# Output projection of a fused fp32 kernel: seven block products over all three input quads, and ten clamps moved to GpSimd

## The chip, the cores and the metric

The kernel runs on one core of a Trainium2 chip. The metric is the device time of one execution in microseconds (us). A core has a matrix engine (TensorE, PE in the rows, with its weight loads as PEld), a vector engine (VectorE, DVE), an activation engine (ScalarE, ACT), a general engine (GpSimd, POOL) and SyncE (SP), whose queue starts the transfers from and to memory. Each engine works through its own instructions in order; semaphores make one engine wait for another.

## The reference

```
attn_out = attention(q_pool, k, v)            # 2 x 8 heads, pooled queries
x = attn_out laid out as (1152 tokens, 512)
h = x @ w_in;  g = elu(h);  x = g @ w_out     # 512 -> 2048 -> 512
xn = x / sqrt(mean(x*x) + 1e-6) * rms_g
g = xn @ w_gate;  val = xn @ w_val            # 512 -> 1536
out = (silu(g) * val) @ w_out                 # 1536 -> 512, the output projection
```

Everything is float32 to full precision. The change concerns the last line, whose left factor is called u below.

## The kernel before

**One product in three.** TensorE multiplies in a reduced format, so each operand is held as a high part and a low part (the rest), and each 128x128 weight block times 128x384 activations takes three matmuls: high·high, low activations·high weights, high activations·low weights (L236 to L238). The activations are kept with the token on the free axis, in three chunks of 384 tokens.

**The output projection.** The 512 output rows are four row blocks m of 128. The inner axis of 1536 is three *quads* of 512, and a quad is four blocks of 128. So the plain product has 4 row blocks x 3 chunks x 3 quads = 36 products of a weight piece (row block, quad) with a quad of u, each 4 x 3 = 12 matmuls. For chunks 0 and 1 and quads 0 and 1 the kernel uses a scheme with seven block products in the place of eight, once for each pair of row blocks, which takes two products off: 34 products, 408 matmuls. The seven need four sums s1 to s4 of weight pieces (`combine_own`, L169) and four differences t1 to t4 of quads of u (`sum_t`, L1159, DVE, 128x1536 each). Every activation that enters TensorE is split: ScalarE casts the high part, DVE (or GpSimd, `lo_pool`) subtracts to get the low part (`split_x`, `split_t`, L1115 to L1125). The buffers xh/xl and th/tl (`tsh`/`tsl` in rows) are used again and again for these parts.

**The weight stream.** `Stream.work` (L101) decodes 68 pieces; the last twelve, W0 to W11 here, belong to the output projection. A piece arrives as 128x512 pairs of 32-bit words, 512 KB, in one of two buffers `wr`. ScalarE turns the low words into a count `we` (L121) and takes the absolute value of the high words into `wm`, a tile in PSUM (L123). DVE clamps `wm` (L132), ors the count in (L134) and sets the sign (L137), which frees the `wr` buffer for the next load. ScalarE casts the high part `wh` (L198), and GpSimd subtracts to get `wl` (L64). `ws.step(i, k)` at a place of the program puts the next k steps of this decode there; `ws.get` puts all that is left until the piece is ready. So the order of all engines' queues is the order of the program's text.

**Sums of pieces.** For earlier weights GpSimd makes the four sums of a pair of pieces (`combine`, L155, four operations on 128x256), ScalarE casts them and GpSimd makes their low part (128x1024). The pairs W8/W9 and W10/W11 before go through `combine_own`: four DVE operations on 128x512 each (L174), which `round_s` splits later (`sumh`/`suml` in rows).

**The order at the end.** First the products that need only W0 to W3, then those with W4 to W7 as they come, then `ws.step(wi + 8, 40)`, which places the rest of the decode, then the plain products with W8 to W11 for chunk 2, and at last the rounds with sums: `sums[1]`, `sums[2]`, `sums[3]`, the pieces W9 and W11 themselves, and `sums[4]`. An evicted product goes to `o` (ScalarE or DVE, L1149) and from there to memory.

Of the kernel before, what the change touches and what calls it, by code (L numbers as in the profile page):

```python
# [22 lines left out]
CH = 384  # L23
# [16 lines left out]
def tile_kernel(ctx: ExitStack, tc: tile.TileContext, qd, kd, vd, w1d, w2d, wgd, wvd, wod, rgd, outd):  # L40
# [33 lines left out]
    class Stream:  # L74
# [26 lines left out]
        def work(self):  # L101
            tail = None
            for i in range(len(self.srcs)):
# [7 lines left out]
                if wide:  # L111
# [8 lines left out]
                    t = self.bank.tile([128, 512], U32, tag="wm", name="wm", bufs=1) if self.bank else w  # L120
                    T.activation(out=e, in_=lo, func=AF.Copy, scale=0.93625 * 2.0 ** -29)  # L121
# [23 lines left out]
                if i in self.keep:  # L145
                    T.copy(self.keep[i], w)
                    yield
# [5 lines left out]
            yield from tail  # L153

# [14 lines left out]
        def combine_own(self, i, a21, a22):  # L169

            s1, s2, s3, s4 = own[i]
            for o, a, b, op in ((s3, s3, a21, ALU.subtract), (s1, a21, a22, ALU.add),
                                (s2, a22, s3, ALU.subtract), (s4, s4, s2, ALU.subtract)):
                V.tensor_tensor(out=o, in0=a, in1=b, op=op)  # L174
                if o is s4:
                    self.own[i] = own[i]
# [14 lines left out]
        def split(self, i, w):  # L191
# [7 lines left out]
            yield  # L199
            lo_pool(l2, w, h2)  # L200
# [73 lines left out]
    last_pieces = [(0, 0), (1, 0), (0, 1), (1, 1), (0, 2), (1, 2), (2, 2), (3, 2), (2, 0), (2, 1), (3, 0), (3, 1)]  # L274
# [257 lines left out]
    def pair_of(i):  # L532
# [8 lines left out]
    ws.place = lambda n: sums_at[n % 2 if n < 8 else 1 if n == 8 else (n - 6) % 3]  # L541
# [434 lines left out]

    class Gate(Branch):
# [9 lines left out]
        def out(self, k, c, p, add=None, into=None):  # L987
            d = u[c][:, self.i + k]
# [22 lines left out]
    def swiglu(i, c, pg, pv, k=4):  # L1011
        s = u[c][:, i]
# [98 lines left out]
    c0, c1 = [at_t(6), at_t(10), at_t(2)], [None, at_x(1), at_x(2)]  # L1111
    c2 = [at_x(0), at_t(6), at_t(10)]
    t1, t2, t3, t4 = at_t(10), at_t(2), at_x(2), at_x(0)

    def split_x(l, w):  # L1115
        h, r = (t[:, 0:4, cs(l)] for t in (xh, xl))
        T.copy(h, w)
        lo_dve(r, w, h)

    def split_t(a, w):  # L1120
        for k in (0,) if a < 9 else (0, 2):
            n = 4 if a < 9 else 2
            h, r = (t[:, (a + k) % 12:(a + k) % 12 + n] for t in (th, tl))
            T.copy(h, w[:, k:k + n])
            lo_dve(r, w[:, k:k + n], h)  # L1125

    quad = lambda c, q: u[c][:, 4 * q:4 * q + 4]
# [182 lines left out]
```

## Time and profile before

| | us |
|---|---|
| median of three executions | 653.56 (655.15, 653.05, 653.56) |
| profiled execution, own time | 653.19 |
| its span | 651.4 |
| PE busy in the span | 643.7 (99%) |
| DVE busy | 542.3 (83%) |
| ACT busy | 468.0 (72%) |
| POOL busy | 443.4 (68%) |
| TensorE's granted clock, mean over the span | 1.00 |

The span is the time between the first and the last recorded instruction; the execution's own time is 1.8 us longer. Rows of the trace name an engine, a line of the kernel, the operation, and the tiles that it writes and reads. A number in brackets behind a row is the idle time of its engine just before, with what ended it. `x2` on a row means two such instructions in a row, with their time together.

### The profile page before, as it was taken

To read this page: it belongs to the slowest core of one execution; us is meant where nothing else is said; L and a number is where in the kernel's file an instruction comes from. 1 tells how busy PE (TensorE), PEld (TensorE's weight loads), DVE (VectorE), ACT (ScalarE), POOL (GpSimd) and SP (SyncE) were. 2 spreads that over 40 slices of the span, in tenths; PEclk is the share of its full clock that TensorE was granted. 3 is DMA by queue.
4 is the path that set the end of the run, shared out by engine and by line. 5 is a ranking of instruction groups with operands and counts; after the bars stand their busy time and mean duration, and the time that the engine had idled before them with its cause. 6 is when DMAs were issued, how large, how long until landed. Compare 5 with 4: busy or idle time off the path is not lost.

```text
span 651.4 us, 11428 instructions
## 1 busy us (share of the span) xinstructions
PE 643.7 (99%) x4073; PEld 637.6 (98%) x4073; DVE 542.3 (83%) x925; ACT 468.0 (72%) x909; POOL 443.4 (68%) x420
## 2 busy tenths in 40 slices
PE   7999999999999999999999999999999999999997
PEld 6999999999999999999999999999999999999997
DVE  6989999999999978987786787688687876768993
ACT  6898889888988968758758668855766745746360
POOL 4989898998999514759686695665989875233200
PEclk9999999999999999999999999999999999999999
DMA  6643536344444202132241232220333422203202
GB/s 182 228 112 127 180 118 201 101 147 138 133 128 128 89 1 69 62 130 98 72 155 65 91 136 93 71 65 32 101 118 107 138 90 98 97 33 105 75 25 73
DMA packets 24165, 68.57 MB, mean 105 GB/s; under 512 B 3316, under 2 KB 5676, under 8 KB 24108
## 3 DMA queue, kind: packets, MB, share of 16 engines
q1 hardware_dynamic: 24108, 67.84, 32.6%
q8 instruction: 32, 0.52, 0.3%
q14 instruction: 25, 0.20, 0.1%
HBM read 60.72 MB, written 2.39 MB: 97 GB/s over the span
## 4 chain that ended last, share of the span: by engine, by line
PE 95%; DVE 2%; issue 1%; DMA 1%; POOL 0%; SPq 0%; DVEq 0%; POOLq 0%
PE b L823 18%; PE b L236 14%; PE b L238 14%; PE b L237 14%; PE s L391 11%; PE o L442 11%; PE t L412 10%; DVE ptl L70 1%; DMA rawq<-in_q_dram 1%; DVE p L395 1%; PE fb L238 0%; PE fb L236 0%; PE fb L237 0%; PE b L791 0%; DVE vd L70 0%
## 5 line engine op out<-in xcount | busy, mean ns | idle before, releaser
L64 POOL TENSOR_TENSOR wl<-wt,wh 128x512 fp32r<-128x512 f32 x68 | 91.4, 1345 | 91.3 <-ACT wh L198 83.0
L70 DVE TENSOR_TENSOR ptl<-t,pth 128x384 fp32r<-128x384 f32 x216 | 106.7, 549 | 2.7 <-ACT pth L422 2.5
L395 DVE TENSOR_SCALAR_CACHE_REDUCE p<-s 128x1152 f32<-128x1152 f32 x72 | 97.3, 1353 | 9.1 <-PE s L391 6.2
L422 ACT CAST pth<-t 128x384 fp32r<-128x384 f32 x216 | 89.0, 485 | 9.5 <-PE t L412 8.9
L400 ACT ACTIVATE p<-p,edge 128x1152 f32<-128x1152 f32 x72 | 90.9, 1263 | 1.2 <-DVE p L395 0.4
L236 PE MATMUL b<-xh,wh 128*128 128x384 f32 x252 | 84.4, 335 | 0.0
L237 PE MATMUL b<-xl,wh 128*128 128x384 f32 x252 | 84.2, 334 | 0.0
L238 PE MATMUL b<-xh,wl 128*128 128x384 f32 x252 | 84.2, 334 | 0.0
L412 PE MATMUL t<-ident,p 128*128 128x128 f32 x648 | 82.6, 273 | 0.0
L442 PE MATMUL o<-pth,vd 128*128 128x256 f32 (+1 forms) x288 | 82.4, 308 | 0.0
L442 PE MATMUL o<-ptl,vd 128*128 128x256 f32 (+1 forms) x288 | 80.2, 301 | 0.0
L412 PEld LDWEIGHTS t<-ident,p 128*128 128x128 f32 x648 | 75.1, 140 | 2.7 <-DVE ptl L70 0.2
L121 ACT ACTIVATE we<-wr 128x512 uint32<-128x512 uint32 x68 | 45.7, 672 | 32.7 <-DMA wr<-in_w_dram 19.9
L391 PE MATMUL s<-kd,qh 128*128 128x384 f32 x240 | 55.8, 345 | 2.7 <-DVE p L395 1.5
L123 ACT ACTIVATE wm<-wr 128x512 f32<-128x512 f32 x63 | 39.4, 626 | 21.1 <-DVE wt L137 21.1
L442 PEld LDWEIGHTS o<-ptl,vd 128*128 128x128 f32 x288 | 54.5, 189 | 0.0
L442 PEld LDWEIGHTS o<-pth,vd 128*128 128x128 f32 x288 | 54.4, 189 | 0.1
L132 DVE TENSOR_SCALAR wm<-wm 128x512 f32<-128x512 f32 x63 | 43.7, 694 | 12.5 <-ACT wm L123 12.4
L236 PE MATMUL b<-gh,wh 128*128 128x384 f32 x144 | 48.4, 336 | 0.0
L238 PE MATMUL b<-gh,wl 128*128 128x384 f32 x144 | 48.1, 334 | 0.0
L237 PE MATMUL b<-gl,wh 128*128 128x384 f32 x144 | 48.1, 334 | 0.0
L236 PEld LDWEIGHTS b<-xh,wh 128*128 128x128 f32 x252 | 47.3, 188 | 0.0
(239 smaller groups left out, 1854.4 us busy)
## 6 DMA issues: line engine op xcount, KB each, us to landing
wr<-in_w_dram SPq DMA_DIRECT2D x32, 512.0 KB
rawq<-in_q_dram SPq DMA_DIRECT2D x15, 576.0 KB
rawk<-in_k_dram SPq DMA_DIRECT2D x28, 288.0 KB
wr<-in_wg_dram SPq DMA_DIRECT2D x12, 512.0 KB
wr<-in_wv_dram SPq DMA_DIRECT2D x12, 512.0 KB
wr<-in_wo_dram SPq DMA_DIRECT2D x12, 512.0 KB
rawv<-in_v_dram SPq DMA_DIRECT2D x16, 288.0 KB
zd<-kd SPq DMA_DIRECT2D x16, 288.0 KB
```

Of the source, the lines that this page charges most:

```text
L64: G.tensor_tensor(out=o, in0=i, in1=f(h), op=ALU.subtract)
L70: V.tensor_tensor(out=o, in0=i, in1=f(h), op=ALU.subtract)
L236: PE.matmul(out, lhsT=wh[:, k, :], rhs=ah, start=first and k == 0, stop=False, skip_group_check=True)
L237: PE.matmul(out, lhsT=wh[:, k, :], rhs=al, start=False, stop=False, skip_group_check=True)
L238: PE.matmul(out, lhsT=wl[:, k, :], rhs=ah, start=False, stop=last and k == 3, skip_group_check=True)
L391: PE.matmul(s[:, m, 0:384], lhsT=a, rhs=b[:, 384 * m:384 * m + 384], start=n == 0, stop=n == len(parts) - 1)
L395: V.tensor_scalar(out=pt, in0=s[:, :, 0:384], scalar1=-0.0625, scalar2=None, op0=ALU.mult, op1=ALU.min, accum_out=st[p][:, 0, TILES[i][4], :])
L400: T.activation(out=pt, in_=pt, func=AF.Exp, scale=-1.0, bias=st[p][:, 0, TILES[i][4], :], accum_out=st[p][:, 1, TILES[i][4], :])
L412: PE.transpose(ps[:, k, :], src[:, 128 * b:128 * b + 128], ident)
L422: T.copy(oh, re(ps))
L442: PE.matmul(self.o[:, 0:self.N], lhsT=v[:, b, :], rhs=(pth, ptl)[u][:, g["buf"], b, g["c0"]:320], start=self.n == 0, stop=self.n == 17)
L823: PE.matmul(out, lhsT=a[x][:, k, :], rhs=b[y][:, k, :], start=first and (k, x, y) == (0, 0, 0), stop=last and (k, x, y) == (1, 1, 0), skip ...
```

## The change

The seven-product scheme is carried to the third quad. As that quad has no partner, it is cut into two halves of two blocks each (`pair`), and a product of a half is 2 x 3 = 6 matmuls. `both` adds a product over a sum of pieces and one over the sum for the halves, 12 + 6 matmuls, in one bank. This takes off 12 matmuls: 396 in the place of 408.

- The halves need sums of the weight pieces W4/W5 and W6/W7, which GpSimd now makes as for the earlier weights (`combine`, then cast and 1024-wide low part): the order of the pieces is changed so that they are neighbours. The pairs W8/W9 and W10/W11 stay with `combine_own` on DVE.
- The differences of u are now `less`: four of 128x1536 and four of 128x768.
- In the last ten pieces (W2 to W11) the clamp runs on GpSimd. The roles of the two tiles are swapped for this: Abs writes the SBUF tile `we`, GpSimd clamps it there, and the count goes to the PSUM tile `wm`.
- DVE's low parts are gathered in a list (`todo`) and placed by `lows()`.
- ScalarE's copies of W8 to W11 (`kept`) stand behind the cast of the piece's high part.
- The stage before the projection takes two more steps of the decode for each product at its end (`run`).

```diff
--- before.py
+++ after.py
...
+                    t = m = self.bank.tile([128, 512], U32, tag="wm", name="wm", bufs=1) if self.bank else w
+                    last = i >= len(self.srcs) - 10
+                    if last:
+                        t, e = e, t
+                    clamp = lambda eng: eng.tensor_scalar(out=f(t), in0=f(t), scalar1=LEAST64, scalar2=MOST64, op0=ALU.max, op1=ALU.min)
+                    count = lambda: T.activation(out=e, in_=lo, func=AF.Copy, scale=0.93625 * 2.0 ** -29)
+                    if not last:
+                        count()
+                        yield
                     T.activation(out=f(t), in_=f(hi), func=AF.Abs, scale=2.0 ** 16)
                     yield
+                    if last:
+                        clamp(G)
+                        yield
+                        count()
+                        yield
...
-                    V.tensor_scalar(out=f(t), in0=f(t), scalar1=LEAST64, scalar2=MOST64, op0=ALU.max, op1=ALU.min)
-                    yield
-                    V.scalar_tensor_tensor(out=t, in0=t, scalar=3, in1=e,
+                    if not last:
+                        clamp(V)
+                        yield
+                    V.scalar_tensor_tensor(out=m, in0=t, scalar=3, in1=e,
                                            op0=ALU.logical_shift_left, op1=ALU.bitwise_or)
                     yield
-                    V.scalar_tensor_tensor(out=w, in0=hi, scalar=0x80000000, in1=t,
+                    V.scalar_tensor_tensor(out=w, in0=hi, scalar=0x80000000, in1=m,
                                            op0=ALU.bitwise_and, op1=ALU.bitwise_xor)
                     self.load(i + 3)
                     yield
...
-                if i in self.keep:
-                    T.copy(self.keep[i], w)
-                    yield
                 n, odd = self.pair_of(i)
+                if after:
+                    yield from after
+                    after = None
                 if n is not None:
-                    tail = chain(tail, self.combine(n, even, w) if n < 18 else self.combine_own(n - 18, even, w)) if odd else tail
+                    if odd and n < 20:
+                        tail = chain(tail, self.combine(n, even, w))
+                    elif odd:
+                        after = self.combine_own(n - 20, even, w)
                     even = w
                 yield
...
             yield
+            if i in self.keep:
+                T.copy(self.keep[i], w)
+                yield
             lo_pool(l2, w, h2)
             self.parts[i] = (h, l)
             self.done += 1
...
-    last_pieces = [(0, 0), (1, 0), (0, 1), (1, 1), (0, 2), (1, 2), (2, 2), (3, 2), (2, 0), (2, 1), (3, 0), (3, 1)]
+    last_pieces = [(0, 0), (1, 0), (0, 1), (1, 1), (0, 2), (2, 2), (1, 2), (3, 2), (2, 0), (2, 1), (3, 0), (3, 1)]
...
         n, odd = divmod(i - 32, 2)
-        return (n + 6, odd) if 2 <= n < 12 else (n + 2, odd) if n >= 16 else (None, odd)
+        return (n + 6, odd) if 2 <= n < 12 else (n + 4, odd) if n >= 14 else (None, odd)
...
-    u.append(u2p.tile([128, 12, CH], F32, name="u2", tag="u2"))
...
+
+    def own_at(i):
+        t = mp.tile([128, 4, 256], F32, tag="sf", name="sf", bufs=1).rearrange("p k c -> p (k c)") if i else flat
...
     b = Gate(11)
-    run([(b, 1), (old, 4), (b, 6), (old, 3)], 10, 12, 1)
+    run([(b, 1), (old, 4), (b, 6), (old, 3)], 10, 12, 2)
     split_u(0, 3, 3, lo_pool)
-    run([(b, 5), (b, 7)], 11, 12, 0)
+    run([(b, 5), (b, 7)], 11, 12, 2)
     split_u(0, 6, 3, lo_pool)
-    run([(b, 2), (b, 8), (b, 4)], 11, 12, 0)
-    split_u(0, 9, 3)
+    run([(b, 2), (b, 8), (b, 4)], 11, 12, 2)
...
+    todo = []
+
+    def lows(n=9):
+        for args in todo[:n]:
+            lo_dve(*args)
...
+        n = w.shape[1]
+        h, r = (t[:, a:a + n, cs(l)] for t in (xh, xl))
         T.copy(h, w)
-        lo_dve(r, w, h)
...
     split_x(0, quad(2, 0))
+    lows()
     run([(b, 3)], 11, 12, 0)
+    split_u(0, 9, 3)
+    split_x(1, quad(2, 1))
     run([(b, 9)], 11, 12, 0)
...
+    def less(o, a, b):
         V.tensor_tensor(out=o, in0=a, in1=b, op=ALU.subtract)
...
-        s = ws.get_own(i)[n - 1]
...
         T.copy(h, s)
-        lo_dve(l, s, h)
...
-    plain = []
+    def both(out, n, i, t, h, first, last):
+        part(out, sums[n, i], t, first, False)
+        part(out, [a[:, 2 * n - 2:2 * n] for a in ws.get_sums(18 + i)], h, False, last)
...
+        part(plain[i], W(i), c2[0], True, False)
+        ws.step(wi + i, 4)
...
+    less(quad(0, 0), quad(1, 0), quad(0, 0))
+    for i in range(2):
+        part(plain[i], W(2 + i), c2[1], False, False)
+        ws.step(wi + 2, 4)
+    for i in range(2):
+        w = W(4 + 2 * i)
+        part(c11[i], w, c0[2][:2], False, False)
+        T.copy(m1[i], c11[i])
+        ws.step(wi + 2 + i, 5)
+        if i:
+            split_t(6, quad(0, 0))
+        else:
+            less(quad(1, 0), quad(1, 1), quad(1, 0))
+        part(plain[i], w, c2[2], False, True)
+        emit_out(i, 2, plain[i])
+        ws.step(wi + 2 + i, 8)
+        plain.append(bank())
+        if i == 0:
+            less(pair(0, 0), pair(1, 0), pair(0, 0))
+            less(pair(1, 0), pair(1, 1), pair(1, 0))
+        part(plain[2 + i], W(5 + 2 * i), c2[2], True, False)
+        ws.step(wi + 2 + i, 8)
+        part(c11[i], W(2 + i), c0[1], False, False)
+        ws.step(wi + 3 + i, 8 if i else 6)
+        part(c11[i], w, c0[2][2:], False, True, 2)
+        emit_out(i, 0, c11[i])
+        ws.step(wi + 4 + 2 * i, 5 if i else 2)
+    lows()
+    split_t(2, pair(0, 0))
+    part(plain[2], W(8), c2[0], False, False)
+    ws.step(wi + 5, 8)
+    part(plain[2], W(9), c2[1], False, True)
+    emit_out(2, 2, plain[2])
+    ws.step(wi + 6, 8)
+    part(plain[3], W(10), c2[0], False, False)
+    ws.step(wi + 8, 60)
     for i in range(2):
         round_s(1, i)
-    split_t(2, quad(1, 1))
+    split_x(2, quad(1, 0))
+    todo[:] = todo[1:3] + todo[:1] + todo[3:]
+    lows(3)
+    less(quad(0, 0), quad(1, 1), quad(0, 0))
+    split_t(10, quad(0, 0))
+    less(pair(0, 0), pair(1, 1), pair(0, 0))
+    part(plain[3], W(11), c2[1], False, True)
...
     for i in range(2):
...
+        round_s(2, i)
+    todo.append(todo.pop(0))
+    lows()
...
-        quads(e[i], sums[1, i], t1, True, False)
+        both(e[i], 1, i, t1, h1, True, False)
+    split_x(1, pair(1, 0))
...
         round_s(3, i)
...
+    less(quad(0, 1), quad(0, 1), quad(0, 0))
+    less(pair(0, 1), pair(0, 1), pair(0, 0))
+    b = [bank(), bank()]
     for i in range(2):
-        quads(b[i], sums[2, i], t2, True, False)
-        V.tensor_tensor(out=x12[i], in0=b[i], in1=x12[i], op=ALU.add)
+        both(b[i], 2, i, t2, h2, True, False)
+        V.tensor_tensor(out=u2s[i], in0=b[i], in1=m1[i], op=ALU.add)
+    split_x(0, quad(0, 1))
+    split_x(1, pair(0, 1), 2)
+    split_t(6, quad(1, 1))
+    split_t(2, pair(1, 1))
+    lows()
+    for i in range(2):
+        both(b[i], 3, i, t3, h3, False, False)
...
         round_s(4, i)
...
+        emit_out(2 + i, 0, b[i], m1[i])
...
+        both(e[i], 4, i, b22, h22, False, True)
+        emit_out(i, 1, e[i], u2s[i])
...
```

On GpSimd's queue, from the last low part of u in the stage before the projection on. `we` is the tile that is clamped, `wl` a piece's low part, `sf` a sum of pieces, `sl` the sums' low part, `tsl` a low part of u. Before, the queue reads:

```order
L166 TENSOR_TENSOR sf<-wt,sf 128x256
L64 TENSOR_TENSOR wl<-wt,wh 128x512
L64 TENSOR_TENSOR sl<-sf,sh 128x1024
L64 TENSOR_TENSOR wl<-wt,wh 128x512 x3
L64 TENSOR_TENSOR tsl<-u_5764,tsh 128x1152 x2
L64 TENSOR_TENSOR wl<-wt,wh 128x512 x8
```

After the change the same stretch reads as follows, up to the clamp and the low part of a piece in the middle of the projection; this piece of the pattern comes once more for the next pair.

```order
L64 TENSOR_TENSOR tsl<-u_5764,tsh 128x1152
L124 TENSOR_SCALAR we<-we 128x512
L64 TENSOR_TENSOR wl<-wt,wh 128x512
L177 TENSOR_TENSOR sf<-wt 128x256
L179 TENSOR_TENSOR sf<-sf,wt 128x256
L181 TENSOR_TENSOR sf<-wt 128x256
L183 TENSOR_TENSOR sf<-wt,sf 128x256
L124 TENSOR_SCALAR we<-we 128x512
L64 TENSOR_TENSOR wl<-wt,wh 128x512
L64 TENSOR_TENSOR sl<-sf,sh 128x1024
```

Between the low parts of single pieces there now stand clamps, four sums of 128x256 for a pair and their 1024-wide low part.

On DVE's queue, before the round with `sums[2]`; `u_5764` and `u_5765` are u of chunks 0 and 1, `suml` the low part of a sum, `kept` a piece that was kept, L1242 the eviction of the second round's bank. Before:

```order
L174 TENSOR_TENSOR u_5889<-wt,kept 128x512
L174 TENSOR_TENSOR kept<-kept,u_5889 128x512
L70 TENSOR_TENSOR suml<-u_5889,sumh 128x512
L70 TENSOR_TENSOR tsl<-u_5765,tsh 128x1536
L70 TENSOR_TENSOR suml<-u_5889,sumh 128x512 x2
L70 TENSOR_TENSOR xl<-u_5765,xh 128x4x384
L70 TENSOR_TENSOR xl<-u_5764,xh 128x4x384
L70 TENSOR_TENSOR tsl<-kept,tsh 128x512 x2
L1242 TENSOR_TENSOR u_5764<-b,u_5764 128x384
```

And after the change, before the same round, whose first product over sums is now evicted at L1309:

```order
L1212 TENSOR_TENSOR u_5764<-u_5765,u_5764 128x1536
L1212 TENSOR_TENSOR u_5764<-u_5765,u_5764 128x768
L70 TENSOR_TENSOR tsl<-u_5764,tsh 128x768 x3
L70 TENSOR_TENSOR suml<-u_5890,sumh 128x512
L70 TENSOR_TENSOR sum_7582<-sf,sum_7582 128x512
L70 TENSOR_TENSOR xl<-u_5765,xh 128x4x384
L70 TENSOR_TENSOR xl<-u_5765,xh 128x2x384
L70 TENSOR_TENSOR over<-kept,over 128x512
L70 TENSOR_TENSOR sum_7630<-kept,sum_7630 128x512
L1212 TENSOR_TENSOR u_5764<-u_5764 128x1536
L1212 TENSOR_TENSOR u_5764<-u_5764 128x768
L1309 TENSOR_TENSOR u_5890<-b,u_5890 128x384
```

Ahead of the eviction there now stand more subtractions in a row: the differences with their halves, and the low parts of the quads, of the halves and of the sums.

## Rows read from the trace of the kernel before

**Rows 1.** The page's first part: engine, busy us, share of the span, instructions.
```profile
PE 643.7 (99%) x4073; PEld 637.6 (98%) x4073; DVE 542.3 (83%) x925; ACT 468.0 (72%) x909; POOL 443.4 (68%) x420
```

**Rows 2.** Windows: the output projection in two stretches.
```profile
core 0: us, PE busy (x) PEld busy (x) DVE busy (x) ACT busy (x) POOL busy (x), PEclk, DMA share, GB/s
577.05:612.00 34.95, 34.95 (x203) 34.95 (x203) 30.43 (x35) 18.77 (x28) 9.67 (x6) 1.00 0.27 93
612.00:647.60 35.60, 35.60 (x208) 35.60 (x206) 27.47 (x37) 12.83 (x19) 2.82 (x2) 1.00 0.12 43
```

**Rows 3.** Timeline of TensorE: start us, us, engine, line, operation, tiles; projection's first, last.
```profile
577.05 0.33 PE L236 MATMUL b<-tsh,wh 128*128 128x384 f32 x1
577.22 0.33 PE L237 MATMUL b<-tsl,wh 128*128 128x384 f32 x1
...
647.59 0.34 PE L238 MATMUL b<-xh,sl 128*128 128x384 f32 x1
```

**Rows 4.** Timeline of DVE: last operation before the projection, and the last eviction.
```profile
574.80 0.56 DVE L994 TENSOR_TENSOR u<-b,u 128x384 f32<-128x384 f32 x1
...
647.97 0.56 DVE L1149 TENSOR_TENSOR o<-b,u 128x384 f32<-128x384 f32 x1 [1.53 <-PE b L238]
```

**Rows 5.** DVE by line and shape, projection: count | busy us, mean ns | idle before.
```profile
L1161 DVE TENSOR_TENSOR u<-u,u 128x1536 f32<-128x1536 f32 x3 | 5.3, 1751 | 0.0
...
L132 DVE TENSOR_SCALAR wm<-wm 128x512 f32<-128x512 f32 x7 | 4.8, 693 | 0.7 <-ACT wm L123 0.7
...
L1242 DVE TENSOR_TENSOR u<-b,u 128x384 f32<-128x384 f32 x2 | 1.1, 554 | 0.0
```

**Rows 6.** Timeline of DVE: low parts in runs, without GpSimd beside them.
```profile
589.33 1.82 DVE L70 TENSOR_TENSOR tsl<-u,tsh 128x768 fp32r<-128x768 f32 x2
...
628.56 1.29 DVE L70 TENSOR_TENSOR suml<-u,sumh 128x512 fp32r<-128x512 f32 x2
629.77 3.42 DVE L70 TENSOR_TENSOR xl<-u,xh 128x1536 fp32r<-128x1536 f32 x2
633.11 1.29 DVE L70 TENSOR_TENSOR tsl<-kept,tsh 128x512 fp32r<-128x512 f32 x2
```

**Rows 7.** Timeline of DVE, beside GpSimd's operations of the next group.
```profile
17.02 1.36 DVE L70 TENSOR_TENSOR vd<-rawv,vd 128x576 fp32r<-128x576 f32 x1
...
585.58 1.76 DVE L70 TENSOR_TENSOR tsl<-u,tsh 128x1536 fp32r<-128x1536 f32 x1 [2.16 <-PE b L238]
...
604.32 0.69 DVE L174 TENSOR_TENSOR kept<-kept,wt 128x512 f32<-128x512 f32 x1
...
604.92 1.78 DVE L174 TENSOR_TENSOR u<-wt 128x512 f32<-128x512 f32 x1
```

**Rows 8.** Timeline of GpSimd at the moments of the group before.
```profile
17.85 1.00 POOL L61 TENSOR_SCALAR qh<-rawq 128x512 fp32r<-128x512 f32 x1
...
586.09 2.41 POOL L64 TENSOR_TENSOR wl<-wt,wh 128x512 fp32r<-128x512 f32 x1 [4.34 <-ACT wh L198]
...
604.36 1.79 POOL L64 TENSOR_TENSOR wl<-wt,wh 128x512 fp32r<-128x512 f32 x1 [1.98 <-ACT wh L198]
```

**Rows 9.** Timeline of GpSimd: operations with no such DVE operation beside them.
```profile
542.34 0.73 POOL L166 TENSOR_TENSOR sf<-wt,sf 128x256 f32<-128x256 f32 x1
...
546.71 1.29 POOL L64 TENSOR_TENSOR wl<-wt,wh 128x512 fp32r<-128x512 f32 x1 [3.63 <-ACT wh L198]
547.96 2.40 POOL L64 TENSOR_TENSOR sl<-sf,sh 128x1024 fp32r<-128x1024 f32 x1
...
618.75 1.30 POOL L64 TENSOR_TENSOR wl<-wt,wh 128x512 fp32r<-128x512 f32 x1 [3.65 <-ACT wh L198]
```

**Rows 10.** GpSimd by line and shape, whole span: the one-input operation of 128x512.
```profile
L61 POOL TENSOR_SCALAR rs<-edge 128x512 f32<-128x512 f32 x1 | 0.6, 617 | 8.8 <-DVE edge L470 8.8
```

**Rows 11.** Timeline of ScalarE: copy of a product out of its bank, cast of a sum.
```profile
579.38 0.48 ACT L1182 COPY u<-b 128x384 f32<-128x384 f32 x1 [1.40 <-PE b L238]
...
620.04 0.62 ACT L1174 CAST sumh<-u 128x512 fp32r<-128x512 f32 x1
```

More of the change, by code (lines that the diff above doesn't have):

```diff
@@ L101, in work @@
         def work(self):
-            tail = None
+            tail = after = None
             for i in range(len(self.srcs)):
@@ L153, in work @@
             yield from tail
+            if after:
+                yield from after
         def combine(self, n, a, b):
@@ L974, in tile_kernel, with block @@
             wi += 4
+    def block(c, i):
+        return u[c][:, i] if c < 2 else u2[i // 8][:, i % 8]
     class Gate(Branch):
@@ L1133, in tile_kernel, with part @@
     wi += 24
-    def quads(out, w, a, first, last):
-        product(out, w, lambda k: a[k], first, last)
+    ws.limit = 20
+    def part(out, w, a, first, last, at=0):
+        wh, wl = w
+        for n, (ah, al) in enumerate(a):
+            k = at + n
+            PE.matmul(out, lhsT=wh[:, k, :], rhs=ah, start=first and n == 0, stop=False, skip_group_check=True)
+            PE.matmul(out, lhsT=wh[:, k, :], rhs=al, start=False, stop=False, skip_group_check=True)
+            PE.matmul(out, lhsT=wl[:, k, :], rhs=ah, start=False, stop=last and n == len(a) - 1, skip_group_check=True)
     def send(m, c, o):
@@ new lines, in round_s @@
+        if n < 3 and i == 0:
+            h, l = ((mp, wp)[n - 1].tile([128, 4, 128], F32R, tag=f"w{a}", name=f"sum{a}", bufs=(WB - NE, NE)[n - 1]) for a in "hl")
+        else:
+            if n == 3:
+                t = mp.tile([128, 1024], F32R, tag="sf", name="sum3", bufs=1) if i else over[0][:, 2048:3072]
+            else:
+                t = wp.tile([128, 1024], F32R, tag="wr", name=f"sum{n}", bufs=2 if wide else 3)
+            h, l = (t[:, a:a + 512].rearrange("p (k c) -> p k c", k=4) for a in (0, 512))
@@ L1174, in round_s @@
         T.copy(h, s)
-        lo_dve(l, s, h)
+        todo.append((l, s, h))
         sums[n, i] = h, l
-    c11 = []
-    for i in range(2):
-        c11.append(bank())
-        quads(c11[i], W(i), c0[0], True, False)
-        T.copy(m1[i], c11[i])
-        ws.step(wi, 4)
-    split_t(6, quad(2, 1))
-    for i in range(2):
-        quads(c11[i], W(2 + i), c0[1], False, False)
-        ws.step(wi, 4)
-    split_t(10, quad(2, 2))
-    plain = [bank() for i in range(2)]
-    quads(plain[0], W(0), c2[0], True, False)
@@ L1213, in tile_kernel @@
[L1213 removed]
+    def both(out, n, i, t, h, first, last):
+        part(out, sums[n, i], t, first, False)
+        part(out, [a[:, 2 * n - 2:2 * n] for a in ws.get_sums(18 + i)], h, False, last)
+    c11, plain = [bank(), bank()], []
+    part(c11[0], W(0), c0[0], True, False)
+    ws.step(wi, 4)
+    lows()
+    part(c11[1], W(1), c0[0], True, False)
+    ws.step(wi, 4)
+    split_x(2, quad(2, 2))
     for i in range(2):
         plain.append(bank())
[L1216 to L1224 removed]
@@ L1236, in tile_kernel @@
-    e, b = [bank() for i in range(2)], [bank() for i in range(2)]
+    split_x(2, quad(1, 0))
[5 more added lines that the diff above has]
+    part(plain[3], W(11), c2[1], False, True)
+    emit_out(3, 2, plain[3])
+    split_t(4, pair(0, 0))
+    for i in range(2):
+        round_s(2, i)
+    todo.append(todo.pop(0))
+    lows()
+    e = [bank(), bank()]
     for i in range(2):
-        quads(e[i], sums[1, i], t1, True, False)
+        both(e[i], 1, i, t1, h1, True, False)
@@ L1243, in tile_kernel @@
+    split_t(6, quad(1, 1))
+    split_t(2, pair(1, 1))
+    lows()
+    for i in range(2):
+        both(b[i], 3, i, t3, h3, False, False)
+        V.tensor_tensor(out=u3s[i], in0=b[i], in1=m1[i], op=ALU.add)
+        emit_out(2 + i, 1, e[i], u3s[i])
+    for i in range(2):
         round_s(4, i)
+    lows()
     for i in range(2):
-        quads(b[i], sums[3, i], t3, False, False)
-        V.tensor_tensor(out=x22[i], in0=b[i], in1=x22[i], op=ALU.add)
-        emit_out(2 + i, 1, e[i], x22[i])
+        part(b[i], W(9 + 2 * i), t4, False, False)
+        part(b[i], W(5 + 2 * i), h4, False, True, 2)
+        emit_out(2 + i, 0, b[i], m1[i])
```

115 lines of the change are left out of this document (36 added, 79 removed).

## Prediction

> **What bounds the kernel now.** I read the share of each engine first, then the windows of the output projection, then the single rows there. TensorE is busy 99% of the span, and DVE is next with 83% [rows 1]. In the projection TensorE has no gap at all: both windows are as long as its busy time, at a granted clock of 1.00 [rows 2]. Its first matmul starts at 577.05 and its 408th, the last, at 647.59, so one goes out every (647.59 − 577.05)/407 = 0.1733 us [rows 3]. Behind the last one only an eviction, a store and the end of the program follow; that eviction starts 0.38 us after it [rows 4], and none of this tail is changed. So the time can fall only by as many matmuls as go, and it rises by whatever makes TensorE wait. The other engines have room on average (DVE 27.47 of the last 35.60 us, GpSimd 2.82) [rows 2], but an average doesn't tell when a thing must be ready. For that I give each matmul a due date: in the changed kernel, matmul n of the projection is due at 577.05 + 0.1733 (n − 1).
>
> **Part 1, the matmuls.** Twelve fewer: 12 x 0.1733 = 2.08 us off, 0.32% of 653.19 us. This is the most that the change can give, since nothing else on TensorE's path is taken away.
>
> **Part 2, what the others must now deliver, and when.** The plain products that used to come first have shrunk, so the sums are wanted earlier: in the new order the first block over sums is matmul 217 (due 614.5). The first product over `sums[3]` is matmul 289, due 577.05 + 288 x 0.1733 = 627.0. It adds into the bank that DVE's first L1309 has to read before, so that eviction must be over by 627.0. I follow the chain that leads to it.
>
> *GpSimd.* Its work now stands between TensorE and the last pieces: clamp, low part, sums, and 1024-wide low parts of sums (the order shows them). Prices: the low part of a piece 1.30 us, 1.25 from start to start; a sum of 128x256 0.73; 1024-wide 2.40 [rows 9]. The clamp (max, then min) on GpSimd has no row. The nearest is GpSimd's other one-input operation of this size with two scalars, 0.617 us [rows 10]; the far end is the two-input operation, 1.30 [rows 9]. Below 0.617 I see no reason to go. I take 0.6, since it has the same number of inputs, scalars and elements, and keep 1.30 for the range. From the clamp of W6 on until that of W11 is done there are 6 clamps (3.6), 5 low parts (6.25), 8 sums (5.9) and two 1024-wide low parts (4.7): 20.45 us.
>
> *Turns.* GpSimd doesn't have this time to itself. Where DVE runs an operation with both inputs in SBUF while GpSimd runs one, one of them stands: at 585.58 DVE's 1.76 us ran unhindered, and GpSimd's low part, begun at 586.09, took 2.41 in the place of 1.30; at 604.32 GpSimd's took 1.79, since DVE's 0.69 us was ahead of it, and then DVE's next, from 604.92, took 1.78 in the place of 0.69, with GpSimd ahead of it [rows 7, 8]. Even a one-input operation of GpSimd took 1.00 instead of 0.62 at 17.85 [rows 8, 10]. The one waiting gets its turn at the end of the other's, some 0.14 before the reported end (585.58 + 1.76 + 1.30 = 588.64 against 588.50). The Trainium skill, page "SBUF — State Buffer", section "Who interferes with whom", says just this against the change: a DVE instruction with two SBUF inputs contends with a GpSimd instruction that reads SBUF, and the later one blocks for the whole of the other. The trace agrees, with the 1.11 and 1.09 us of these rows; without that rule the clamp would be free and the sum would be the first rival's, 651.2.
>
> The clamp of W6 can start at 577.0, when DVE's low part after the last gate product ends (last gate eviction at 574.80, 0.56 [rows 4], then cast and low part). Until the clamp of W11 DVE has seven operations of the colliding kind in its queue: low parts of 1152 (1.36), 1536 and 1536, and the differences of 1536, 1536, 768 and 768. With 1.75 for 1536 [rows 5] and 0.95 for 768 [rows 6] that is 10.25, less a quarter of a microsecond each for the two early handovers: 8.5. So the clamp of W11 ends at 577.0 + 20.45 + 8.5 = 605.95.
>
> *DVE behind it.* DVE then has, in this order: the four own sums of W8/W9 (0.69 and then 0.605 a step, 2.55), or and sign of W11 (1.4), a low part of 1536 (1.67), a turn of GpSimd for the low part of W11 (1.15), and the four own sums of W10/W11 (2.55). From 605.8 that ends at 615.1. After this DVE has work without a pause up to the eviction: six low parts of 512 at 0.605 = 3.63; five low parts and two differences of 768 at 0.865 = 6.06; one low part and two differences of 1536 at 1.67 = 5.0; and the eviction, 0.55 [rows 5]. (The steps are those of operations in a row: 1.29 − 0.69, 1.82 − 0.95, 3.42 − 1.75 [rows 6].) That is 15.25, and with two short waits for casts 15.4: the eviction ends at 630.5. TensorE wants it at 627.0 and stands **3.5 us**.
>
> **What hides, and what comes later.** The ten clamps that leave DVE (0.693 each [rows 5]) are worth nothing by themselves, since TensorE waits for DVE nowhere in the projection today. TensorE will have smaller stalls before, as pieces W8 to W11 come late by the same chain, but they are part of the 3.5 and not added: DVE's chain runs on through them. Behind the third round DVE has some 6.1 us of work for 36 matmuls (6.24 us), so the lag doesn't grow. The copies moved behind the casts, and the extra steps of the decode in the gate stage (or and sign of W5 come earlier, where DVE's margin is about 0.8 us), cost nothing as long as that margin stands.
>
> **The sum.** −2.08 + 3.5 = +1.4 us. On the profiled execution's own 653.19 us that makes 654.6 us. (It lies 0.37 below the median of the runs shown, 653.56, well within their spread.) A measurement of this kernel can tell about 0.3%, 2 us, from no change, so the forecast reads "no difference".
>
> **Rivals.**
>
> *A. The turns are hidden.* If DVE's operations happen to fall where GpSimd waits for ScalarE or a load, GpSimd keeps its 20.45 us and the clamp of W11 is done by 597.5. What then starts DVE's last run is ScalarE: its cast of the first own sum stands in its queue behind the copy of W9's product, matmul 192, due 610.15. A copy starts 0.42 after the last matmul (579.38 against the 12th, 578.96) and takes 0.48, 0.4 to the next; a cast takes 0.62 [rows 11]. So the run starts at 611.6, the eviction ends at 627.0, and nothing is late: 653.19 − 2.08 + 0.1 = 651.2. For it speaks that GpSimd has long gaps today, up to 4.3 us before one low part [rows 8]; against it that the collisions seen fell in this very stretch, and that GpSimd's work there is now more than twice as much.
>
> *B. Slower: the clamp on GpSimd is dear.* It is on the chain six times, and it makes DVE wait too. Each 0.1 us more adds 0.6 to the clamp of W11, and the same to the 3.5. At 0.8 the sum is 655.8, at 1.0 it is 657.0; at the far end, 1.30, it is +4.2, 658.8. Past +0.3% it comes from a clamp of 0.7 us on. For it speaks that two-scalar max and min have no row on GpSimd; against it the 0.617.
>
> *C. The change takes no matmuls off, or other ones.* The order of TensorE's queue has 12 matmuls fewer, all in the projection. I give it no chance.
>
> **How the numbers follow.** The forecast's mechanism gets 0.50 (its own range 653.4 to 655.8, since each turn may be missed or taken twice), A 0.23 (650.9 to 651.8), B 0.27 (655.5 to 658.8). The range from 651.0 to 656.9 holds the forecast, A but its edge, and the cheaper half of B, about 8 in 10. Faster by over 0.3% (below 651.2) is half of A, less what it gives at its edge: 0.09. Slower by over 0.3% (above 655.15) is most of B and a quarter of the forecast's case less its overlap: 0.34. Within 0.3%: 0.57.
>
> **What the profile after will show.** The clamp on GpSimd: a row of 128x512 with max and min of about 0.62; near 1 it is B. Turns: low parts on GpSimd of 2 us and more and differences on DVE above 1.75 between 580 and 606; if they stay at 1.30 and 1.75 it is A. The own sums of W10/W11 end near 615, and the low parts and differences behind them run without gaps to the first L1309 near 630. TensorE shows idle time before matmuls that wait for DVE, a few us in all, the last just before the first product over `sums[3]`. Wrong would be the whole argument if TensorE stands earlier and for something else, above all in the gate stage, where the decode was moved forward, or for a load of a piece.

## The result, and the profile after

The changed kernel takes 659.12 us (median of six, 658.50 to 660.21) against 653.92 us before (six, 652.68 to 655.86). The ratio is 1.0078, with a 95% interval of 1.0059 to 1.0097: slower by 0.8%, where 654.6 us, "no difference", was forecast, with a range up to 656.9. The profiled execution took 659.11 us, its span is 657.3.

The first part of the page after the change, and the projection in two windows (busy us of each engine, then granted clock, DMA share, GB/s):

```profile
PE 644.1 (98%) x4061; PEld 635.3 (97%) x4061; DVE 542.8 (83%) x916; ACT 473.4 (72%) x914; POOL 479.4 (73%) x440
```

```profile
577.05:612.00 34.95, 32.09 (x184) 31.45 (x183) 24.20 (x25) 15.92 (x24) 34.24 (x21) 1.00 0.22 72
612.00:653.60 41.60, 38.59 (x215) 36.68 (x213) 33.18 (x39) 16.31 (x24) 3.49 (x2) 1.00 0.12 44
```

TensorE has its twelve matmuls fewer. But where it had no gap [rows 2], it now stands in both windows, and GpSimd is busy in 34.24 of the first 34.95 us, where it had 9.67. DVE is the less busy one in that window (24.20 against 30.43): it waits for GpSimd.

TensorE's first and last matmul of the projection, and what it waited for (us in total, times, longest):

```profile
576.97 0.33 PE L1189 MATMUL b<-tsh,wh 128*128 128x384 f32 x1
...
653.52 0.34 PE L1191 MATMUL b<-tsh,over 128*128 128x384 f32 x1
```

```profile
PE b L1189 <- ACT spare L1253: 1.7, 1, 1.7
PE b L1189 <- DVE u L1309: 1.3, 1, 1.3
PE b L1190 <- DVE xl L70: 1.2, 1, 1.2
PE b L1191 <- DVE suml L70: 1.2, 2, 0.7
PE b L1191 <- POOL wl L64: 0.4, 1, 0.4
PE b L1189 <- ACT sumh L1226: 0.2, 1, 0.2
```

396 matmuls at 0.1733 us need 395 x 0.1733 = 68.45 us between the first and the last start; there are 653.52 − 576.97 = 76.55. So TensorE loses 8.1 us, of which the list names 6.0. Most of the rest lies right behind the same waits: of the 1.54 us between the starts at 590.49 and 592.03, for example, the wait is 1.20 and the usual step 0.17, and the next step is 0.28. −2.08 + 8.1 is +6.0, and the last matmul starts 5.93 later than before [rows 3].

The first thing to look at is GpSimd. Its timeline from the clamp of W10 on:

```profile
606.39 1.92 POOL L124 TENSOR_SCALAR we<-we 128x512 f32<-128x512 f32 x1
608.27 1.29 POOL L64 TENSOR_TENSOR wl<-wt,wh 128x512 fp32r<-128x512 f32 x1
609.53 1.93 POOL L124 TENSOR_SCALAR we<-we 128x512 f32<-128x512 f32 x1
```

The clamp takes 1.92 us by itself (1.91 to 1.93 in every row without a turn). It was put at 0.6, after the multiplication of [rows 10], with 1.30 as the far end. DVE behind it: its or for W10, which waits for the clamp, then the own sums of W10/W11 and the eviction that TensorE waits for:

```profile
608.34 0.70 DVE L146 SCALAR_TENSOR_TENSOR wm<-we,wm 128x512 uint32<-128x512 uint32 x1 [4.06 <-POOL we L124]
...
615.65 1.77 DVE L191 TENSOR_TENSOR kept<-kept,wt 128x512 f32<-128x512 f32 x1
...
618.66 0.69 DVE L191 TENSOR_TENSOR kept<-kept,sf 128x512 f32<-128x512 f32 x1
...
634.20 0.55 DVE L1309 TENSOR_TENSOR u<-b,u 128x384 f32<-128x384 f32 x1
```

The own sums end at 619.35 (forecast: 615.1), and from there DVE works without a pause to the end of the eviction at 634.75: 15.4 us, as worked out.

### The profile page after: what moved, and what is told of

It reads as the page before. It is cut to its first block, busy times and chain, and to the rows that moved or that the text cites. A ratio compares the mean times of both kernels' runs of the same rounds, so it can differ in the third digit from the quotient of the medians.

```text
span 657.3 us, 11429 instructions
## 1 busy us (share of the span) xinstructions
PE 644.1 (98%) x4061; PEld 635.3 (97%) x4061; DVE 542.8 (83%) x916; ACT 473.4 (72%) x914; POOL 479.4 (73%) x440
## 4 chain that ended last, share of the span: by engine, by line
PE 85%; DVE 8%; POOL 3%; issue 2%; DMA 1%; ACT 1%; SPq 0%; DVEq 0%; POOLq 0%
PE b L843 17%; PE s L411 11%; PE b L256 10%; PE b L258 10%; PE b L257 10%; PE o L462 10%; PE t L432 9%; PE b L1189 2%; PE b L1190 2%; PE b L1191 2%; DVE ptl L70 2%; POOL we L124 1%; DVE xl L70 1%; POOL tsl L64 1%; DVE p L415 1%
## 5 line engine op out<-in xcount | busy, mean ns | idle before, releaser
L256 PE MATMUL b<-xh,wh 128*128 128x384 f32 x212 | 71.1, 335 | 0.0
L257 PE MATMUL b<-xl,wh 128*128 128x384 f32 x212 | 70.8, 334 | 0.0
L258 PE MATMUL b<-xh,wl 128*128 128x384 f32 x212 | 70.8, 334 | 0.0
L125 ACT ACTIVATE we<-wr 128x512 uint32<-128x512 uint32 x58 | 38.8, 669 | 26.8 <-DMA wr<-in_w_dram 19.4
L64 POOL TENSOR_TENSOR gl<-eg,gh 128x384 fp32r<-128x384 f32 x35 | 37.5, 1093 | 12.7 <-ACT gh L289 12.7
L149 DVE SCALAR_TENSOR_TENSOR wt<-wr,wm 128x512 uint32<-128x512 uint32 x63 | 43.2, 686 | 3.5
L124 DVE TENSOR_SCALAR wm<-wm 128x512 f32<-128x512 f32 x53 | 36.8, 694 | 11.1 <-ACT wm L129 10.9
```

What stands on the lines that cost most here:

```text
L64: G.tensor_tensor(out=o, in0=i, in1=f(h), op=ALU.subtract)
L256: PE.matmul(out, lhsT=wh[:, k, :], rhs=ah, start=first and k == 0, stop=False, skip_group_check=True)
L257: PE.matmul(out, lhsT=wh[:, k, :], rhs=al, start=False, stop=False, skip_group_check=True)
L258: PE.matmul(out, lhsT=wl[:, k, :], rhs=ah, start=False, stop=last and k == 3, skip_group_check=True)
```

## The experiments

**The multiplication in the place of the clamp.** Everything stays, only GpSimd's operation is the one whose price had been used.

```diff
+times = lambda: G.tensor_scalar(out=f(t), in0=f(t), scalar1=1.0, scalar2=1.0, op0=ALU.mult, op1=ALU.mult)
-                        clamp(G)
+                        times()
```

> The changed kernel, with a multiplication by 1 twice in the place of max and min in the ten GpSimd operations; the clamp itself is left out of these ten pieces, all else is the same. Theory 1 (the price of max and min on GpSimd is the one term of the sum that was wrong): the ten rows fall from 1.92 to about 0.62 us, the last own sums end near 615 and the first L1309 near 630.5, and the time is that of the forecast's sum, 654.6 (653.9 to 655.5). Rival 2 (the place of the operation, in the tile that ScalarE has just written, or its being in place, makes it dear, whatever it computes): the rows stay at 1.9 and the time at 659. Rival 3 (DVE's last run is started by something else): rows of 0.62, but the time stays above 657.

Measured: 654.84 us (654.15 to 656.67), ratio 1.003 (1.002 to 1.004) against 653.24. The operations on GpSimd for W6, W10 and W11, then DVE's or for W10, its own sums of W10/W11 and the eviction:

```profile
574.92 2.14 POOL L125 TENSOR_SCALAR we<-we 128x512 f32<-128x512 f32 x1
...
602.85 0.64 POOL L125 TENSOR_SCALAR we<-we 128x512 f32<-128x512 f32 x1
...
604.84 0.62 POOL L125 TENSOR_SCALAR we<-we 128x512 f32<-128x512 f32 x1
```

```profile
603.51 0.70 DVE L147 SCALAR_TENSOR_TENSOR wm<-we,wm 128x512 uint32<-128x512 uint32 x1 [2.79 <-POOL we L125]
...
610.84 1.79 DVE L192 TENSOR_TENSOR kept<-kept,wt 128x512 f32<-128x512 f32 x1
...
613.86 0.69 DVE L192 TENSOR_TENSOR kept<-kept,sf 128x512 f32<-128x512 f32 x1
...
629.40 0.55 DVE L1310 TENSOR_TENSOR u<-b,u 128x384 f32<-128x384 f32 x1
```

The last of the ten ends at 605.46 (forecast 605.95), the own sums at 614.55 (615.1), the eviction at 629.95 (630.5), the whole at 654.84 (654.6; this profiled execution took 654.32). From its first matmul of the projection, at 576.47, to its last, at 648.73, TensorE loses 3.8 us (3.5 forecast). So the other terms of the sum came out near what was forecast, and the clamp's price is what was wrong. Rivals 2 and 3 fall.

**What GpSimd's operations cost.** Behind the last eviction of the kernel before, one after the other, each twice (the second round alike to 0.01 us). The listing is shortened; A, B and C are 128x512 pieces of a tile in SBUF:

```diff
...
+    two = lambda o, i, p, q: G.tensor_scalar(out=o, in0=i, scalar1=LEAST64, scalar2=MOST64, op0=p, op1=q)
+    for n in range(2):
+        two(B, A, ALU.mult, ALU.mult); two(A, A, ALU.mult, ALU.mult)
+        two(B, A, ALU.max, ALU.min); two(A, A, ALU.max, ALU.min)
+        two(B, A, ALU.mult, ALU.min); two(B, A, ALU.add, ALU.mult)
+        G.tensor_scalar(out=B, in0=A, scalar1=LEAST64, scalar2=None, op0=ALU.max)
+        G.tensor_scalar(out=B, in0=A, scalar1=LEAST64, scalar2=None, op0=ALU.mult)
+        two(B[:, 0:256], A[:, 0:256], ALU.max, ALU.min)
+        G.tensor_tensor(out=B, in0=A, in1=C, op=ALU.subtract)
+        G.tensor_copy(B, A)
+        V.tensor_scalar(out=A, in0=B, scalar1=LEAST64, scalar2=MOST64, op0=ALU.max, op1=ALU.min)
```

> The kernel before with a list of GpSimd operations of 128x512 behind its last eviction, where no other engine works, so its time tells nothing. Theory 1: max with min is 1.92 us in place or not, and multiplications are 0.62 in place or not; max alone would then be about 1.2 if the price is paid for each max or min, or 1.9 if one of them is enough. Rival 2 (in place is dear): both kinds cost 0.62 into another tile and 1.92 in place.

The rows of GpSimd in the order of the list (multiplication twice, into another tile and in place; max and min, into another tile and in place; multiplication and min; add and multiplication; then one scalar, max and multiplication; 128x256; subtraction; copy), and DVE's clamp in SBUF:

```profile
649.06 0.62 POOL L1260 TENSOR_SCALAR u<-u 128x512 f32<-128x512 f32 x1
649.76 0.62 POOL L1260 TENSOR_SCALAR u<-u 128x512 f32<-128x512 f32 x1
650.46 1.91 POOL L1260 TENSOR_SCALAR u<-u 128x512 f32<-128x512 f32 x1
652.46 1.91 POOL L1260 TENSOR_SCALAR u<-u 128x512 f32<-128x512 f32 x1
654.45 1.92 POOL L1260 TENSOR_SCALAR u<-u 128x512 f32<-128x512 f32 x1
656.46 0.62 POOL L1260 TENSOR_SCALAR u<-u 128x512 f32<-128x512 f32 x1
```

```profile
657.16 1.50 POOL L1268 TENSOR_SCALAR u<-u 128x512 f32<-128x512 f32 x1
658.74 1.49 POOL L1269 TENSOR_SCALAR u<-u 128x512 f32<-128x512 f32 x1
660.32 1.07 POOL L1260 TENSOR_SCALAR u<-u 128x256 f32<-128x256 f32 x1
661.47 1.26 POOL L1271 TENSOR_TENSOR u<-u 128x512 f32<-128x512 f32 x1
662.79 0.61 POOL L1272 COPY u<-u 128x512 f32<-128x512 f32 x1
```

```profile
663.44 0.43 DVE L1273 TENSOR_SCALAR u<-u 128x512 f32<-128x512 f32 x1 [15.13 <-POOL u L1272]
```

In place or not makes no difference for the two kinds tried both ways; the operation does: 0.62 for two multiplications or an add with one, 1.91 for max with min, and as much when only one of the two is a min. A single multiplication costs 1.49, more than two. My guess for max alone, 1.2 or 1.9, missed (1.50).

**The third quad alone.** The clamp of all pieces back on DVE, in PSUM.

```diff
-                    last = i >= len(self.srcs) - 10
+                    last = False
```

> The changed kernel with the clamp of all pieces on DVE, in PSUM, as before; the seven products over the third quad stay. Theory 1: GpSimd loses ten operations of 1.92 us, DVE gains ten of 0.69. From 577 on that is six on each; DVE had some 6.6 us without work between 600 and 608 in the changed kernel, so its last run starts some 3 to 4 us earlier than 619.3: 655 (654 to 656). Rival 2 (DVE's own sum of work is the limit, and the clamp is simply needed elsewhere): 657 or more, with DVE without gaps from 577 on. Rival 3 (with the clamp gone from GpSimd nothing is late): 651.5.

Measured: 657.87 us, ratio 1.0084 (1.0063 to 1.0104). Rival 2 holds: DVE hardly stands any more. Windows, columns as above:

```profile
577.00:600.00 23.00, 22.62 (x131) 22.30 (x130) 21.99 (x19) 10.73 (x15) 16.73 (x10) 1.00 0.21 64
600.00:612.00 12.00, 9.53 (x47) 9.21 (x46) 10.86 (x16) 7.08 (x12) 7.80 (x6) 0.86 0.28 105
612.00:640.00 28.00, 26.79 (x155) 26.50 (x154) 27.80 (x30) 15.71 (x22) 3.02 (x2) 1.00 0.06 22
```

DVE is busy 21.99 of 23, 10.86 of 12 and 27.80 of 28 us. Its own sums end at 617.72 and the eviction at 633.13, only 1.6 us earlier than in the changed kernel. I had counted on the 6.6 us in which DVE stood there; six clamps and the turns with GpSimd took most of it. So the third quad with the clamp left where it was brings as large a loss, and by the times the two places of the clamp can't be told apart (1.0084 on DVE, 1.0078 on GpSimd, intervals that overlap): at 1.92 us GpSimd's queue is late, at 0.69 us DVE's own.

**The clamp alone.** The kernel before with the last ten clamps on GpSimd, tiles swapped as in the change, no other edit.

> The kernel before with only the clamp of the last ten pieces moved to GpSimd, tiles swapped as in the changed kernel. Theory 1 (a dear clamp hurts only where GpSimd's queue has no room left): GpSimd is busy 12.5 of 70.6 us in the projection there and gains 11.5, no piece becomes late: 653.6, within 1 us. Rival 2 (the clamp's 1.92 us in each piece's own chain, Abs, clamp, count, or, sign, next load, makes pieces late by itself): 655 to 658, with TensorE waiting for pieces W8 to W11.

Measured: 653.94 us, ratio 1.0012 (1.0001 to 1.0022). TensorE waits for nothing in the projection there, and GpSimd has gaps before its operations:

```profile
605.94 2.05 POOL L124 TENSOR_SCALAR we<-we 128x512 f32<-128x512 f32 x1 [0.89 <-ACT we L129]
612.71 1.52 POOL L64 TENSOR_TENSOR wl<-wt,wh 128x512 fp32r<-128x512 f32 x1 [4.72 <-ACT wh L210]
```

An operation of 1.92 us costs nearly nothing where the queue has room; in the changed kernel it costs, where the sums of the third quad stand in that queue too and GpSimd is busy 34.24 of 34.95 us.

**Without the first differences.** The multiplications again, and the first four differences of u left out.

```diff
-    less(quad(0, 0), quad(1, 0), quad(0, 0))
...
-            less(quad(1, 0), quad(1, 1), quad(1, 0))
...
-            less(pair(0, 0), pair(1, 0), pair(0, 0))
-            less(pair(1, 0), pair(1, 1), pair(1, 0))
```

> The changed kernel with multiplications in the place of the ten clamps, and with the first four differences of u left out (two of 128x1536, two of 128x768), so that neither the clamp nor these differences are computed. Theory 1 (GpSimd's turns with DVE's two-input operations are what remains of the loss): GpSimd gets through some 4.4 us earlier, DVE's last run starts when ScalarE has cast the first own sum, near 611.6, in the place of 614.5, and TensorE is hardly late: 651.4 (651.1 to 652.0), which also shows the 2.08 us of the twelve matmuls. Rival 2 (something else holds the last run, a load or ScalarE): 653.5 or more.

Measured: 651.5 us, ratio 0.9973 (0.9962 to 0.9984), faster than before. GpSimd's last of the ten, and ScalarE's first cast of an own sum:

```profile
600.89 1.08 POOL L125 TENSOR_SCALAR we<-we 128x512 f32<-128x512 f32 x1 [0.20 <-ACT we L130]
```

```profile
610.27 0.48 ACT L1203 COPY o<-b 128x384 f32<-128x384 f32 x1 [2.99 <-issue]
610.64 0.62 ACT L1227 CAST sumh<-u 128x512 fp32r<-128x512 f32 x1
```

The last of the ten ends at 601.97 in the place of 605.46, 3.5 us earlier (4.4 expected), DVE's own sums end at 610.47, and what then starts the last run is ScalarE's cast, done at 611.26 (611.6 in the first rival). That is the first rival's course and its time. TensorE waits for nothing in the projection and loses 0.4 us there, so nearly all of the 2.08 us is left; this kernel leaves out work, though, and is no faster version. The four differences are work of DVE as well as turns with GpSimd, so the run doesn't part these two; but with the multiplications alone DVE stood waiting for GpSimd in that stretch (2.79 us in the row at 603.51 above).

**Is there a better place for the clamp?** First all ten on DVE, but in the SBUF tile, where one took 0.43 us; then W2 to W5 on GpSimd and W6 to W11 on DVE in SBUF.

```diff
+                    here = False                                  # first version
+                    here = last and i < len(self.srcs) - 6        # second version
-                    if last:
+                    if here:
                         clamp(G)
                         yield
+                    if last:
                         count()
...
-                    if not last:
+                    if not here:
                         clamp(V)
```

> The changed kernel with the ten clamps on DVE, but in the tile in SBUF (tiles still swapped), where such an operation of DVE took 0.43 us behind everything else, against 0.69 in PSUM. Theory 1 (with the clamp on DVE, DVE's own sum of work sets the end): six clamps at 0.26 less are 1.6 us, so 656.3 (655.5 to 657). Rival 2 (the clamp in SBUF takes turns with GpSimd, as DVE's two-input operations do): no gain or a loss, 657.9 or more, with rows of the clamp of 1 us and longer beside GpSimd's operations.

> The changed kernel with the clamps of W2 to W5 on GpSimd, as changed, and those of W6 to W11 on DVE in SBUF. Theory 1: GpSimd's 1.92 us are then paid in the gate stage, where its queue has room, and DVE is spared four clamps there; from 577 on it is as with all ten on DVE in SBUF: that time, or up to 1 us less, 655.3 to 656.3. Rival 2 (GpSimd's backlog at 577 comes from the clamps of W2 to W5 already): no better than the changed kernel, 659.

Measured: 658.91 us for the first (ratio 1.0092, 1.007 to 1.0115) and 655.66 us for the second (1.0042, 1.0027 to 1.0058). In the first, DVE's clamp takes turns with GpSimd:

```profile
583.57 0.49 DVE L125 TENSOR_SCALAR we<-we 128x512 f32<-128x512 f32 x1
...
593.62 2.62 DVE L125 TENSOR_SCALAR we<-we 128x512 f32<-128x512 f32 x1
...
604.90 2.25 DVE L125 TENSOR_SCALAR we<-we 128x512 f32<-128x512 f32 x1
```

Of 0.43 us alone it becomes 2.62 beside a low part of GpSimd. So rival 2 of that run holds. The Trainium skill, page "SBUF — State Buffer", section "Who interferes with whom", has that a tensor_scalar can enter a mode with two ports when its operands meet certain conditions, and can then contend with GpSimd. These rows agree with it.

The second came out inside its expectation: four clamps are paid in the gate stage, where GpSimd had room. That is in part luck, for the range was built on some 656.3 for the first version, which came to 658.91. The two differ by 3.2 us, and not by 1 at most. In the profiled executions (658.82 and 655.33) the projection takes 74.92 and 73.49 us from its first matmul's start to its last's, so 1.4 us of the difference arises there; 1.6 more stand before its first matmul (577.86 against 576.22), though TensorE waits for nothing in either between 400 us and there. No run shows that this part comes from the clamps.

**TensorE's longest wait.** In the second version TensorE waited 2.8 us for ScalarE's copy into `spare`, which stood behind a count (L126) that waited for DVE. Two edits: the copy is placed before that count; then also the last two differences of u and the low parts that hang on them behind the L1311 evictions.

```diff
-        ws.step(wi + 2 + i, 5)
+        ws.step(wi + 2 + i, 16 if i else 5)
...
-        ws.step(wi + 2 + i, 8)
+        ws.step(wi + 2 + i, 8 if i else 5)
...
-        ws.step(wi + 3 + i, 8 if i else 6)
+        ws.step(wi + 3 + i, 8 if i else 0)
...
-        ws.step(wi + 4 + 2 * i, 5 if i else 2)
+        ws.step(wi + 4 + 2 * i, 5 if i else 0)
```

```diff
-    less(quad(0, 1), quad(0, 1), quad(0, 0))
-    less(pair(0, 1), pair(0, 1), pair(0, 0))
     b = [bank(), bank()]
...
+    less(quad(0, 1), quad(0, 1), quad(0, 0))
+    less(pair(0, 1), pair(0, 1), pair(0, 0))
     split_x(0, quad(0, 1))
     split_x(1, pair(0, 1), 2)
+    lows()
     split_t(6, quad(1, 1))
     split_t(2, pair(1, 1))
-    lows()
...
+    lows()
     for i in range(2):
         round_s(4, i)
```

> The version with the clamps of W2 to W5 on GpSimd and of W6 to W11 on DVE in SBUF, with one thing moved: five decode steps are placed behind ScalarE's copy into spare, so that this copy no longer stands behind a count (L126) that waits for DVE. TensorE waited 2.8 us for that copy near 602, its longest wait. Theory 1 (DVE's run to the first L1311 sets the end, whatever TensorE waits for before): that wait goes, another of the same size appears before the third round, and the time stays, 655.5 (655.0 to 656.0). Rival 2 (the copy is the cause of the delay): 653.0.

> The same, and besides the last two differences (2.6 us on DVE) and the low parts that hang on them placed behind the two L1311 evictions, those of the last round behind the third round's evictions. Theory 1: DVE's run to the first L1311 is 2.6 us shorter, but TensorE's second round still waits for the low parts of its sums near 624 and ends near 629.8, so only about 0.8 us come off: 654.8 (654.2 to 655.4). Rival 2 (with the copy moved, TensorE is ready at 627 and the eviction alone is late): 653.0.

Measured: 656.08 us with the copy moved (ratio 1.0037, 1.0026 to 1.0048) and 655.68 us with both (1.0028, 1.0015 to 1.0041); the version that they start from had 655.66. All waits of TensorE in the projection, in the version that they start from, and two windows of it (columns as above):

```profile
PE b L1191 <- ACT spare L1255: 2.8, 1, 2.8
```

```profile
606.00:608.00 2.00, 2.00 (x9) 2.00 (x8) 1.97 (x4) 1.51 (x3) 0.00 (x0) 0.62 0.25 92
608.00:610.00 2.00, 2.00 (x8) 2.00 (x8) 1.80 (x4) 2.00 (x3) 1.33 (x1) 0.52 0.01 4
```

The waits with the copy moved, and with both edits the one that takes the place of the wait for L1311:

```profile
PE b L1191 <- DVE u L1311: 1.2, 1, 1.2
PE b L1193 <- DVE suml L70: 1.2, 2, 0.7
PE b L1193 <- POOL wl L64: 0.6, 1, 0.6
PE b L1191 <- ACT sumh L1228: 0.2, 1, 0.2
```

```profile
PE b L1191 <- DVE u L1319: 0.8, 1, 0.8
```

The wait of 2.8 us is gone, and with it the low clock behind it (0.62 and 0.52 in the two windows, some 1.5 us more); 3.2 us of other waits stand in their place. The trace with the copy moved is of the slowest of its eight executions (658.03), which came late to the projection (first matmul at 579.02 against 576.22). Within the projection the two are alike: TensorE needs 73.49 us from its first start to its last in the one and 73.41 in the other, and DVE's first L1311 ends 54.7 and 54.6 us behind TensorE's first start. So the longest wait of TensorE was worth nothing, since DVE's run behind it set the end. The second edit was expected to give 0.8 us and gave nothing that can be told (655.68 against 656.08, intervals that overlap). Its trace shows the projection at 72.92 us: counted from TensorE's first start, the first of the two evictions is over 2.6 us earlier, the second then waits for TensorE (1.5 us), and the work that was moved is waited for later, at L1319. No version that does the whole work beats the kernel before.

## Why the prediction was wrong, step by step

- **The bound and the first term held.** TensorE's matmuls bound the kernel and the twelve are worth about 2.08 us: 651.5 us against 653.47 is what came when nothing else was late, in a kernel that leaves out work.
- **The chain held, with one link named wrongly.** GpSimd's clamps, then or and sign, the own sums, DVE's run of 15.4 us, the first L1309, TensorE. But DVE's part hangs on the clamp of W10, not on that of W11: its or for W10 waits for GpSimd (at 603.51 with multiplications, at 608.34 in the changed kernel), and from there on it works through; W11's clamp is done before DVE asks for it (605.46 against 607.84, and 611.46 against 612.53). With the price that was used, the sum gave 605.95, 615.1, 630.5 and 654.6; measured with that price: 605.46, 614.55, 629.95 and 654.84.
- **The turns held.** With multiplications the operation of W6 was done at 577.06 already; it had begun at 574.92, not at 577.0, and stood in a turn. From there to 605.46 GpSimd needed 28.4 us for what is left of its own work, 20.45 − 0.6 = 19.85 us, so 8.5 us went into turns, as put in. That W6 was ahead makes up for the 0.5 us by which the end came before the forecast.
- **The failed step is one term: the clamp at 0.6 us, "since it has the same number of inputs, scalars and elements".** It measured 1.92. The bound was wrong too: 1.30, the two-input operation, was called the far end, and the true price lies beyond it. The rows of the trace told prices of multiplications, additions and subtractions on GpSimd, and none of a comparison; number of inputs and elements did not carry over.
- **The slope was overstated.** The second rival put six clamps on the chain, and six times 1.30 us more should have moved the time by 7.8 us; it moved from 654.84 to 659.12, 4.3. As DVE's part hangs on W10's clamp, only five are on the chain, 6.5 us. And the turns didn't stay the same: from the start of W6's clamp to the end of W10's GpSimd needed 28.57 us with multiplications (574.92 to 603.49) and 32.88 with clamps (575.43 to 608.31), 4.3 more, so 2.2 us less went into turns. A dearer term also shifts what it collides with.
- **Rivals.** What came is the second rival's mechanism with a price outside its range, so its 0.27 and the whole range (up to 656.9) were too low. That 659.12 lies so near to the 658.8 which it gave for 1.30 us is chance: the price was higher and the slope lower. The first rival did not come, but its time was met to 0.3 us when four differences, and with them their collisions, were left out.
- **What was costed at nothing.** The clamps taken off DVE were called worth nothing by themselves: right for the kernel before (1.0012 with them on GpSimd), but with the third quad DVE is full when they are on it (657.87 us). The gate stage stayed without a wait of TensorE, as forecast.

## What to carry to other kernels

Before an operation is moved to another engine, find a row of that very operation on that engine; the nearest by shape can be off by a factor of three, and where no row exists the far end should not be the dearest row at hand; here the price was three times the near one. A saving on the engine that bounds a kernel pays only if every helper's last deadline still holds: give due dates and follow the one chain that misses first. And of an engine's waits, the longest need not be worth anything: when the one of 2.8 us was moved away here, others behind it took its place.

## What the runs showed of the hardware

- GpSimd, 128x512 in SBUF: two multiplications 0.62, add with multiplication 0.62, max with min 1.91, multiplication with min 1.92, one multiplication alone 1.49, max alone 1.50, subtraction of two inputs 1.26, copy 0.61 us.
- DVE's clamp of 128x512 takes 0.43 us in SBUF and 0.69 in PSUM [rows 5], but the one in SBUF waits for GpSimd's operations (up to 2.62 us) and the one in PSUM does not: with the clamp on DVE in PSUM its rows from 548 us on stay between 0.68 and 0.70, beside GpSimd's operations too.
- TensorE's granted clock fell after a standstill: with the clamp on DVE no matmul started between 603.61 and 606.41, and the clock of the window from 606 was 0.53, near the lower of its two levels, 1.2 of 2.4 GHz; it was back at 1.00 from 610 on (windows as above). At the low clock a matmul started every 0.32 us in the place of 0.17. In the version with W6 to W11 on DVE in SBUF no matmul started between 602.05 and 605.15, and there the low clock came only from 606.5 on, with seven matmuls at full pace between.

```profile
604.00:606.00 2.00, 0.00 (x0) 0.00 (x0) 1.27 (x3) 1.57 (x4) 2.00 (x2) 1.00 0.28 86
606.00:608.00 2.00, 1.59 (x5) 1.59 (x6) 1.91 (x4) 0.79 (x2) 0.99 (x1) 0.53 0.70 274
608.00:610.00 2.00, 2.00 (x9) 2.00 (x8) 1.97 (x4) 2.00 (x3) 0.00 (x0) 0.61 0.00 0
610.00:612.00 2.00, 2.00 (x14) 2.00 (x13) 1.88 (x4) 1.11 (x4) 0.82 (x1) 1.00 0.26 97
```

In the changed kernel, where no matmul started between 604.30 and 606.29, it stayed at 1.00. With the clamp on DVE in PSUM this didn't set the end: TensorE waited 1.2 us for DVE's L1309 afterwards.
